# DeltaNet blocks and a mixture of experts on one core: five products on single heads in 64x64 tiles, and bulk transfers spread over the block

## The chip, the cores and the metric

The kernel runs on one core of a Trainium2 chip. The metric is the time of one execution on the device in microseconds; below, the median of several runs. The engines are called PE (matrix products, with PEld its weight loads), DVE (vector), ACT (scalar), POOL (GpSimd) and SP (which here only issues transfers). Each executes its instructions in the order of the program; they meet through semaphores.

## The reference, cut to what matters

```python
# q, k, v: (4, 8, 768, 48); beta: (4, 8, 768)
k_n = k / (norm(k) + 1e-6)
for t in range(S):
    y[t]  = q[t] @ state                       # state: 48 x 48 for each of 32 heads
    v_old = state.T @ k_n[t]
    state = state + beta[t] * outer(k_n[t], v[t] - v_old)
x = y as rows of 384                           # 3072 tokens
logits = x @ w_gate                            # 8 experts
expert = argmax(logits); gate_w = softmax(logits)[expert]
for e in range(8):                             # the 80 tokens of largest gate_w
    out[tok] = gate_w[tok] * (relu(x[tok] @ w1[e]) @ w2[e])
```

All other rows of the output are zero. All data are float32.

## The kernel before, in words

The sequence of 768 is cut into 12 chunks of 64 positions. `for j in range(NC)` (L766) makes one block of work of each; all 32 heads go through it together. A head has three numbers (e, p, g): e and p are 0 or 1, g is 0 to 7, and the tables of the chunk are laid out by them. In most operands one partition half (0 to 63, 64 to 127) holds heads of one e or one p, the other half those of the other.

Block j carries several chunks at different stages, so that the engines have work while the chain of the states runs:

- Chunk j, the chain. `chain_ks` (K times the state SB), `R` on DVE (V minus that, L474), `chain_tr` (the inverse factor YF times R), `UB` on DVE (the result times gam, L485), `chain_ku` (K times UB, added to the state in `S_ps`), and the copies of the state into SB on ACT (L504). Outputs: `chain_qs` (Q times the old state) and `chain_pu` (P times UB) add up in one PSUM tile, `x_out` copies it (L517) and stores it to `x_rows`, `out_t` transposes it and ACT copies it to xT (L528); `logits` of chunk j follow in block j+1.
- Chunk j+1, the inverse of a 64x64 triangular matrix per head, put together from 16x16 diagonal blocks: `place_y` (ACT), `merge_f` (B1 times XB), FB on DVE (L424), `merge_y`, the YF copies (L435), `merge_p`, the PB copies (L449, L451), `merge_u`, the YF copies of L464. `place_x(j+2)` (ACT, L408) makes XB for the next block.
- Chunks j+2 to j+5, the diagonal blocks. `gram(j+5)` on PE makes B1 and PT (L335, L340). `store(j+4)` writes B1's diagonal blocks to DRAM in eight transfers (L348), `fetch` brings them back as NT with one 16x16 block on each partition (L352). In odd blocks POOL inverts those of two chunks, `solve([j+3, j+4])` (L367 to L380). In the next, even block `put` writes the result to DRAM (L391) and `spread` brings it back as XD and YD, in four transfers (L402), for two chunks. XD is what place_x needs.
- Loads: `load_v(j+2)`, `load_kq(j+6)` (Q and K transposed, in two halves of 512 KB, into the buffer that chunk j has used), `load_k(j+8)`; in the last blocks `clear` (zeros into the output) and `load_first` (the first expert weights into free KQ buffers). `scale_v` (L319) multiplies V on POOL, `squares` and `norm` give the norms of K.
- `fill(us)` puts pieces of the routing work (`gate`, `gate_top`) between the others on DVE.

Nothing reorders this: the order of the calls in the block is the order on each engine, and SP takes its transfers in that order too, waiting for each one's semaphores before the next is issued.

Merge_f, chain_ks, chain_qs, chain_ku and chain_pu treat two heads with one product. The stationary side stacks both heads on 128 partitions, and the right side holds the two heads' 48 columns block by block, with zeros in between: 96 columns. For that SB, UB and XB carry an extra axis, whose other half is zeroed once at the start (L674). A float32 product counts as two matmul records, so such a product over 32 heads is 32 records. `chain_tr` and `gram` go through `tiles` (L222) instead: one head at a time on a quarter (64x64) of the array, the four quarters in turn. Every call of `mm` has line L234 in the profile, so products are told apart by their tiles.

After the blocks come the routing (thresholds, ranks, indices; 266 to 306 us in the profiled execution) and the eight experts (306 to 366 us), which the change leaves as they are.

Of the kernel before, what the change touches and what calls it, by code (L numbers as in the profile page):

```python
# [32 lines left out]
def _layout(inputs):  # L33
# [13 lines left out]
    out["vtok"] = vb.transpose(4, 0, 5, 3, 1, 2, 6).reshape(NC, 128, 16 * D)  # L47
# [30 lines left out]
def kernel(  # L78
# [85 lines left out]
    def load_first(s):  # L164
        t = KQ[s].rearrange("p g k w -> p (g k w)").rearrange("p (c f) -> p c f", f=F)
        for k in range(KW):
            e, c = divmod(s * KW + k, DK)
            w_t.setdefault(2 * e, []).append(t[:, k])
            nc.sync.dma_start(t[:, k], w1[e, :, c * F : c * F + F])

    with ExitStack() as actx:
# [19 lines left out]
        XB = blk.tile([128, NB, 2, 48], F32, name="XB")  # L191
        YB = blk.tile([128, NB, 2, 2, 16], F32, name="YB")
        FB = blk.tile([128, 2, 4, 2, 64], F32, name="FB")
        YF = fixed("YF", 2, [128, 2, 8, 64])
        PB_ = blk.tile([128, 2, 8, 32], F32, name="PB")
        SB = blk.tile([128, NQ, 2, 2, D], F32, name="SB")
        UB = blk.tile([128, NB, 2, D], F32, name="UB")
# [21 lines left out]
        PAIRS = [(a, 4 * c + ql) for a in range(2) for ql in range(4) for c in range(2)]  # L219
        XPAIRS = [(a, 4 * c + 2 * r + q) for a in range(2) for c in range(2) for q in range(2) for r in range(2)]  # L220

# [11 lines left out]
        def mm(out, lhsT, rhs, acc=False):  # L233
            nc.tensor.matmul(out, lhsT=lhsT, rhs=rhs, start=not acc, stop=not acc, skip_group_check=True)  # L234

# [51 lines left out]
        def norm_of(bs, ss):  # L287
# [22 lines left out]
            for i, c in enumerate(bs):  # L310
                for e in range(2):
                    for h in range(2):
                        nc.gpsimd.tensor_copy(nvs[hs(h), c, 8 * e : 8 * e + 8].rearrange("r (q p) -> r p q", p=2),
                                              nv[hs(e), i, :, h].rearrange("r (p q) -> r p q", p=2))
# [27 lines left out]
        def store(c, engs=(nc.sync, nc.sync)):  # L342
            if ok(c):
                ad = a_dram[c % 4].rearrange("(e g b r w) -> e b r g w", e=2, g=NB, b=4, r=16)
                for n in range(8):
# [58 lines left out]
        def place_x(c, es=(0, 1)):  # L404
            if ok(c):
                for e in es:
                    for i in range(3):
                        nc.scalar.mul(XB[hs(e), :, e, 16 * i : 16 * i + 16], XD[hs(e), :, c % 2], bmask[hs(e), i : i + 1])  # L408

# [8 lines left out]
        def merge_f(c, ps):  # L418
            if ok(c):
                for p, g in PAIRS:  # L420
                    mm(ps[hs(g // 4), p, 96 * (g % 4) : 96 * (g % 4) + 96].rearrange("r (e w) -> r e w", e=2),
                       B1[c % B1n][:, slot(p, g)], XB[:, slot(p, g)])
                for p in range(2):
                    nc.vector.copy_predicated(FB[:, p].rearrange("r g e w -> r (g e) w")[:, :, 0:48],  # L424
                                              mask48.bitcast(I32).unsqueeze(1).to_broadcast([128, 8, 48]),
                                              ps[:, p, :384].rearrange("r (g w) -> r g w", w=48))

        def merge_y(c, ps):
            if ok(c):
                for m in range(8):  # L430
                    for e in range(2):
                        mm(ps[hs(e), 0, 64 * m : 64 * m + 64], FB[:, m // 4, m % 4, e], YB[:, 8 * e + m].rearrange("r h b w -> r (h b w)"))
# [5 lines left out]
        def merge_p(c, ps, eng=None):  # L438
            if ok(c):
                for m in range(8):  # L440
                    for e in range(2):
                        for h in range(2):
                            k = 64 * h + 32 * (m % 2)
                            mm(ps[k : k + 32, 1, 128 * e + 32 * (m // 2) : 128 * e + 32 * (m // 2) + 32],
                               FB[64 * h + 32 : 64 * h + 64, m // 4, m % 4, e, 0:32], YF[c % 2][64 * h + 32 : 64 * h + 64, e, m, 32:64])
# [7 lines left out]
        def merge_u(c, ps):  # L453
            if ok(c):
                for m in range(8):
                    for e in range(2):
                        for h in range(2):
                            k = 64 * h + 32 * (m % 2)
                            mm(ps[k : k + 32, 0, 128 * e + 32 * (m // 2) : 128 * e + 32 * (m // 2) + 32],
                               FB[64 * h : 64 * h + 32, m // 4, m % 4, e, 0:32], PB_[64 * h : 64 * h + 32, e, m])  # L460
# [6 lines left out]
        def chain_ks(c, ps):  # L467
            if ok(c) and c > 0:
                kq = KQ[c % KQn]
                for e, g in PAIRS:  # L470
                    mm(ps[hs(g // 4), e, 2 * D * (g % 4) : 2 * D * (g % 4) + 2 * D].rearrange("r (p d) -> r p d", p=2),
                       kq[:, g, 0, hs(e)], SB[:, g, e])
                for e in range(2):
                    nc.vector.tensor_tensor(out=R[:, 8 * e : 8 * e + 8], in0=VT[c % VTn][:, 8 * e : 8 * e + 8],  # L474
                                            in1=ps[:, e, : 8 * D].rearrange("r (g d) -> r g d", d=D), op=Alu.subtract)

        def chain_tr(c, ps):
            if ok(c):
# [3 lines left out]
                                         Y[hs(g // 4), e, pq(p, g)], r[hs(g // 4), 8 * e + 2 * (g % 4) + p]))  # L482
                for e in range(2):
                    bt = gam[hs(e), c].rearrange("r (g c) -> r c g", c=2).unsqueeze(3).to_broadcast([64, 2, 8, D])
                    nc.vector.tensor_tensor(out=UB[hs(e), :, e].rearrange("r (g c) d -> r c g d", c=2),  # L485
                                            in0=ps[hs(e), :, : 8 * D].rearrange("r c (g d) -> r c g d", d=D), in1=bt, op=Alu.mult)

        def chain_qs(c, ps):
            if ok(c) and c > 0:
                kq = KQ[c % KQn]  # L490
                for e, g in XPAIRS:
                    mm(ps[hs(g % 4 // 2), g // 4, 4 * D * (g % 2) : 4 * D * (g % 2) + 4 * D]
                       .rearrange("r (p e d) -> r e p d", p=2, e=2)[:, e], kq[:, g, 1, hs(e)], SB[:, g, e],
                       acc=e + g % 2 > 0)

        def chain_ku(c):
            if ok(c) and c < NC - 1:
                kb = KT[c % KTn]
                for g in range(NQ):
                    for p in range(2):  # L500
                        mm(S_ps[hs(p, D), g // 4, 2 * D * (g % 4) : 2 * D * (g % 4) + 2 * D].rearrange("r (e d) -> r e d", e=2),
                           kb[:, slot(p, g)], UB[:, slot(p, g)], acc=True)
                for p in range(2):
                    nc.scalar.copy(SB[hs(p, D), :, :, p].rearrange("r (b g) e d -> r b (g e) d", b=2),  # L504
                                   S_ps[hs(p, D), :, : 8 * D].rearrange("r b (g d) -> r b g d", d=D))

        def chain_pu(c, ps):
            if not ok(c):
                return
            for p, g in XPAIRS:  # L510
                o = 4 * D * (g % 2) + 2 * D * p
                mm(ps[hs(g % 4 // 2), g // 4, o : o + 2 * D].rearrange("r (e d) -> r e d", e=2), PT[c % PTn][:, slot(p, g)], UB[:, slot(p, g)],
                   acc=c > 0)

        def x_out(c, ps, b):
            if ok(c):
                nc.scalar.copy(x_t[c % 2][:, b].rearrange("r h d -> r (h d)"), ps[:, b, : 8 * D])  # L517
# [137 lines left out]
        zr = out.rearrange("(a q r) d -> a q r d", q=128, r=2)  # L655

        def clear(a):
            if a < zr.shape[0]:
                nc.sync.dma_start(zr[a], zero.unsqueeze(1).to_broadcast([128, 2, DM]))
# [14 lines left out]
        for t in (YF[0], YF[1], XB, YB, SB, UB):  # L674
# [27 lines left out]
        nc.vector.tensor_copy(FB.rearrange("r p q e w -> r (p q e) w"), eye.unsqueeze(1).to_broadcast([128, NB, 64]))  # L702
# [49 lines left out]

        def gated(b, m0, m1):
# [12 lines left out]
        for j in range(NC):  # L766
            a, b2, m2 = pms[j % 2], pms[1 - j % 2], pms[2]
            store(j + 4)
            load_v(j + 2)
            place_y(j + 1)  # L770
            fetch(j + 4)
            if j % 2:
                scale_v(j + 1)
                squares(j + 6, SQ[0])
                squares(j + 7, SQ[1])
                scale_v(j + 2)
                solve([j + 3, j + 4])
            elif j == 0:
# [266 lines left out]
```

## Time and profile before

| | |
|---|---|
| median of 3 runs | 381.9 us (379.48 to 385.86) |
| the profiled execution | 376.49 us, its span 374.8 us |
| mean clock granted to PE | 0.858 |
| before block 1 (its chain_ks) | 0 to 71 us |
| blocks 1 to 11 | 71 to 266 us |
| PE waiting for XB (ACT, L408) | 14.9 us, 7 times |
| PE waiting for KQ to land | 14.0 us, 3 times |
| PE waiting with no releaser seen ("issue") | 9.5 us, 7 times |
| SP queue waiting for inv_blocks (L402) / for POOL's XY (L391) | 25.7 / 19.7 us |

A line of a timeline gives start, length, engine, line, operation, the tile written and those read, and how many instructions were merged; in brackets, how long the engine had been idle before and who released it. SPq and ACTq are transfers being issued by SP and ACT; their landing comes later. A line of the table by stretches gives each engine's busy time.

### The profile page before, as it was taken

Reading aid. Unit: us, or ns where it says so; the run is one execution under the profiler, and the core shown is the slowest. Engines: PE = TensorE matmul, PEld = TensorE weight load, DVE = VectorE, ACT = ScalarE, POOL = GpSimd, SP = SyncE. Lnnn points to the kernel's source line nnn. Section 1 sums busy time; section 2 is a strip of 40 time slices with the busy share of each in tenths; the row PEclk is TensorE's granted clock in tenths of the full one; section 3 lists DMA queues with packets and bytes.
Section 4 is the critical chain, followed back from the end, with each engine's and each line's share of the span. In section 5 each row is a group of like instructions: output and inputs, shape, how many; then the busy total and the mean of one; then the engine's idle time right before and its main releaser. Section 6 shows DMA issues by size and latency. Waiting matters only on the chain. (4 is left out here: it accounts for less than half of the span.)

```text
span 374.8 us, 16506 instructions
## 1 busy us (share of the span) xinstructions
PE 272.8 (73%) x7313; PEld 241.0 (64%) x7313; DVE 199.2 (53%) x489; ACT 159.7 (43%) x352; POOL 150.0 (40%) x377
## 2 busy tenths in 40 slices
PE   6334737748798978979987987697301579799994
PEld 2333427647697867978886977687301249799993
DVE  3699835518434969585464467575887720011111
ACT  3202557455566675757667487771200001111120
POOL 8366128905870588058705880100340052110001
PEclk9855687969698999698998599998855599999999
DMA  7786865396359646763468259927799527961000
GB/s 301 207 307 224 86 159 149 128 200 191 88 175 203 190 97 188 151 201 59 118 170 265 79 122 321 311 85 242 255 429 429 218 58 266 420 233 32 18 17 26
DMA packets 75879, 69.52 MB, mean 185 GB/s; under 512 B 57248, under 2 KB 65440, under 8 KB 73504
## 3 DMA queue, kind: packets, MB, share of 16 engines
q1 hardware_dynamic: 70080, 65.03, 55.8%
q10 hardware_dynamic: 4960, 1.48, 1.9%
q0 software_dynamic: 768, 1.97, 1.8%
q8 instruction: 57, 0.93, 1.0%
q14 instruction: 14, 0.11, 0.1%
HBM read 53.32 MB, written 15.14 MB: 183 GB/s over the span
## 5 line engine op out<-in xcount | busy, mean ns | idle before, releaser
L234 PE MATMUL pm<-KQ 48*64 48x128 f32 x704 | 29.0, 313 | 24.0 <-DMA KQ<-in_kqt_dram 14.0
L234 PE MATMUL pm<-SB,KQ 128*64 128x96 f32 x704 | 40.3, 275 | 6.0 <-ACT YF L464 5.0
L234 PEld LDWEIGHTS pm<-SB,KQ 128*64 128x64 f32 x704 | 35.8, 157 | 9.7 <-ACT YF L464 6.6
L234 PEld LDWEIGHTS pm<-KQ 48*64 48x64 f32 x704 | 23.6, 155 | 26.3 <-DVE XY L378 11.8
L319 POOL TENSOR_TENSOR VT<-VT,nvs 128x768 f32<-128x768 f32 x12 | 17.7, 1474 | 49.5 <-DMA VT<-in_vtok_dram 49.2
L408 ACT ACTIVATE XB<-XD,cst 64x256 f32<-64x256 f32 x72 | 31.2, 496 | 8.5 <-DMA XD<-inv_blocks 8.1
L376 POOL TENSOR_TENSOR tmpTrue<-XY,NT 128x28 f32<-128x28 f32 (+13 forms) x84 | 30.9, 368 | 6.1
L234 PE MATMUL pm<-XB,B 128*64 128x96 f32 x384 | 22.3, 279 | 14.9 <-ACT XB L408 14.9
L1003 ACT ACTIVATE hT<-hp 128x320 f32<-128x320 f32 x16 | 7.0, 437 | 61.3 <-PE hp L1000 61.3
L435 ACT COPY YF<-pm 64x256 f32<-64x256 f32 x48 | 17.6, 366 | 34.1 <-PE pm L234 31.3
L378 POOL TENSOR_TENSOR XY<-XY,tmpTrue 128x28 f32<-128x28 f32 (+13 forms) x84 | 28.0, 334 | 6.6
L234 PEld LDWEIGHTS pm<-XB,B 128*64 128x64 f32 x384 | 19.8, 160 | 16.1 <-ACT XB L408 15.6
L970 DVE COPY xTe<-xp 128x240 f32<-128x240 f32 x8 | 3.3, 408 | 50.1 <-PE xp L968 50.1
L1011 PE MATMUL yp<-hT,w 128*64 128x80 f32 x768 | 29.1, 234 | 0.4 <-issue 0.4
L424 DVE COPY_PREDICATED FB<-cst,pm 128x384 f32<-128x384 int32 x24 | 12.8, 588 | 30.5 <-PE pm L234 30.5
L1011 PEld LDWEIGHTS yp<-hT,w 128*64 128x64 f32 x768 | 27.5, 137 | 2.1 <-issue 1.0
L984 POOL DMA_INDIRECT out_dram<-y,idx_s x8 | 7.4, 920 | 52.2 <-DVE y L983 52.2
L485 DVE TENSOR_TENSOR UB<-pm,gam 64x768 f32<-64x768 f32 x24 | 22.9, 955 | 3.2 <-PE pm L234 2.7
L474 DVE TENSOR_TENSOR R<-VT,pm 128x384 f32<-128x384 f32 x22 | 11.2, 551 | 23.9 <-PE pm L234 9.4
L335 DVE TENSOR_TENSOR B<-pm,ngam 128x512 f32<-128x512 f32 x22 | 15.1, 690 | 15.0 <-PE pm L234 14.0
L414 ACT ACTIVATE YB<-YD,cst 64x256 f32<-64x256 f32 x48 | 21.7, 498 | 0.5
L464 ACT COPY YF<-pm 32x256 f32<-32x256 f32 x24 | 8.7, 363 | 24.6 <-DVE YF L464 15.5
(177 smaller groups left out, 595.8 us busy)
## 6 DMA issues: line engine op xcount, KB each, us to landing
w<-in_w_dram SPq DMA_DIRECT2D x12, 1536.0 KB, 12.3
KQ<-in_kqt_dram SPq DMA_DIRECT2D x6, 1024.0 KB, 7.6
KQ<-in_kqt_dram SPq DMA_DIRECT2D x12, 512.0 KB, 5.6
KQ<-in_w_dram SPq DMA_DIRECT2D x12, 512.0 KB, 6.3
VT<-in_vtok_dram SPq DMA_DIRECT2D x12, 384.0 KB, 4.1
x_rows<-x SPq DMA_DIRECT2D x12, 384.0 KB, 5.1
out_dram<-zero SPq DMA_DIRECT2D x12, 384.0 KB, 4.7
KT<-in_ktok_dram SPq DMA_DIRECT2D x11, 384.0 KB, 7.8
```

The lines of the kernel that those rows point to most:

```text
L234: nc.tensor.matmul(out, lhsT=lhsT, rhs=rhs, start=not acc, stop=not acc, skip_group_check=True)
L319: eng.tensor_tensor(out=V, in0=V, in1=nvs[:, c].unsqueeze(2).to_broadcast([128, NB, D]), op=Alu.mult)
L335: nc.vector.tensor_tensor(out=own(B1[c % B1n], h), in0=pv[:, 0], in1=own(ngam[:, c].unsqueeze(2).to_broadcast([128, NB, 64]), h), op=Alu.mult)
L376: eng.tensor_tensor(out=tv, in0=X[:, :, t + 1 :, t : t + 1].to_broadcast(sh), in1=NT[:, :, 0:t, t].unsqueeze(2).to_broadcast(sh), op=Alu.mult)
L378: eng.tensor_tensor(out=X[:, :, t + 1 :, 0:t], in0=X[:, :, t + 1 :, 0:t], in1=tv, op=Alu.add)
L408: nc.scalar.mul(XB[hs(e), :, e, 16 * i : 16 * i + 16], XD[hs(e), :, c % 2], bmask[hs(e), i : i + 1])
L414: nc.scalar.mul(YB[hs(h), :, h, b], YD[hs(h), :, c % 2], bmask[hs(h), 2 * b + 1 : 2 * b + 2])
L424: nc.vector.copy_predicated(FB[:, p].rearrange("r g e w -> r (g e) w")[:, :, 0:48], mask48.bitcast(I32).unsqueeze(1).to_broadcast([128, 8, ...
L435: nc.scalar.copy(YF[c % 2][hs(h), e].rearrange("r m (b x w) -> r m b x w", b=2, x=2)[:, :, :, 1], ps[hs(e), 0].rearrange("r (m h b w) -> r ...
L474: nc.vector.tensor_tensor(out=R[:, 8 * e : 8 * e + 8], in0=VT[c % VTn][:, 8 * e : 8 * e + 8], in1=ps[:, e, : 8 * D].rearrange("r (g d) -> ...
L485: nc.vector.tensor_tensor(out=UB[hs(e), :, e].rearrange("r (g c) d -> r c g d", c=2), in0=ps[hs(e), :, : 8 * D].rearrange("r c (g d) -> r ...
L1011: nc.tensor.matmul(yp[r, d * cap : (d + 1) * cap], lhsT=w2_t[f][:, d * 128 + 64 * n : d * 128 + 64 * n + 64], rhs=hT[:, f, :], start=(f == ...
```

## The change

It has four parts.

1. The five products go through `tiles`, one head at a time, 48 columns wide: 64 records for 32 heads. SB, UB and XB lose the extra axis. SB gets two buffers, used in turn by the chunks. V, FB and the sums in PSUM are laid out to suit. The operations on DVE and ACT that fill these tiles cover 128 partitions at once.
2. `chain_qs` is cut in two halves of 16 heads; the first is issued before chain_tr, the second after chain_pu.
3. Of the eight stores of a chunk's diagonal blocks, four are issued by ACT. `fetch` follows right behind `load_v`; `put` moves from behind chain_qs to the start of the block; `spread` moves behind chain_pu. In odd blocks `scale_v` no longer stands around squares and ahead of solve; both chunks are scaled in even blocks.
4. The two halves of a KQ load are issued in different places: the first half late in block j, the second early in block j+1; the expert weights that go into the KQ buffers likewise. `clear` works on pieces of half the size, three in each block from block 4 on, in three places, instead of two in each block from block 6 on.

```diff
-        XB = blk.tile([128, NB, 2, 48], F32, name="XB")
+        XB = blk.tile([128, NB, 48], F32, name="XB")
-        SB = blk.tile([128, NQ, 2, 2, D], F32, name="SB")
-        UB = blk.tile([128, NB, 2, D], F32, name="UB")
+        SB = fixed("SB", 2, [128, 2, NQ, D])
+        UB = blk.tile([128, NB, D], F32, name="UB")
...
+        def xmm(row, ps, ops, acc, heads=HEADS):
+
+            seen = set()
+
+            def emit(e, p, g):
+                t = g % 4 // 2, e
+                o = D * (4 * (g // 4) + 2 * (g % 2) + p)
+                mm(ps[hs(t[0]), e, o : o + D], *ops(e, p, g), acc=acc or t in seen)
+                seen.add(t)
+
+            tiles(lambda e, p, g: (row(e, p), g % 4 // 2), emit, heads)
...
-        def place_x(c, es=(0, 1)):
-            if ok(c):
-                for e in es:
-                    for i in range(3):
-                        nc.scalar.mul(XB[hs(e), :, e, 16 * i : 16 * i + 16], XD[hs(e), :, c % 2], bmask[hs(e), i : i + 1])
+        def place_x(c):
+            if ok(c):
+                for i in range(3):
+                    nc.scalar.mul(XB[:, :, 16 * i : 16 * i + 16], XD[:, :, c % 2], bmask[:, i : i + 1])
...
-                for p, g in PAIRS:
-                    mm(ps[hs(g // 4), p, 96 * (g % 4) : 96 * (g % 4) + 96].rearrange("r (e w) -> r e w", e=2),
-                       B1[c % B1n][:, slot(p, g)], XB[:, slot(p, g)])
+                tiles(lambda e, p, g: (e, g // 4),
+                      lambda e, p, g: mm(ps[hs(g // 4), e, 48 * pq(p, g) : 48 * pq(p, g) + 48],
+                                         B1[c % B1n][hs(e), slot(p, g)], XB[hs(e), slot(p, g)]))
...
-                for e in range(2):
-                    bt = gam[hs(e), c].rearrange("r (g c) -> r c g", c=2).unsqueeze(3).to_broadcast([64, 2, 8, D])
-                    nc.vector.tensor_tensor(out=UB[hs(e), :, e].rearrange("r (g c) d -> r c g d", c=2),
-                                            in0=ps[hs(e), :, : 8 * D].rearrange("r c (g d) -> r c g d", d=D), in1=bt, op=Alu.mult)
+                for h in range(2):
+                    bt = own(gam[:, c].unsqueeze(2), h).to_broadcast([128, 8, D])
+                    nc.vector.tensor_tensor(out=own(UB, h), in0=ps[:, h, : 8 * D].rearrange("r (m d) -> r m d", d=D), in1=bt, op=Alu.mult)
...
-        def chain_qs(c, ps):
+        def chain_qs(c, ps, k):
             if ok(c) and c > 0:
                 kq = KQ[c % KQn]
-                for e, g in XPAIRS:
...
+                xmm(lambda e, p: p, ps, lambda e, p, g: (kq[hs(p, D), g, 1, hs(e)], SB[c % 2][hs(p, D), e, g]), k > 0,
+                    [hd for hd in HEADS if hd[0] ^ hd[1] != k])
...
+        def load_kq_or_w(c, p):
+            if KQn <= c < NC:
+                load_kq(c, parts=(p,))
+            elif NC < c < NC + KQn:
+                load_first(c - NC - 1, (p,))
...
         for j in range(NC):
             a, b2, m2 = pms[j % 2], pms[1 - j % 2], pms[2]
-            store(j + 4)
+            store(j + 4, (nc.sync, nc.scalar))
             load_v(j + 2)
+            fetch(j + 4)
+            load_kq_or_w(j + 5, 1)
+            clear(3 * j - NC)
+            if j % 2 == 0:
+                put([j + 2, j + 3])
             place_y(j + 1)
-            fetch(j + 4)
             if j % 2:
-                scale_v(j + 1)
                 squares(j + 6, SQ[0])
                 squares(j + 7, SQ[1])
+                solve([j + 3, j + 4])
+            else:
+                if j == 0:
+                    squares(6, SQ[0], nc.scalar)
+                scale_v(j + 1)
                 scale_v(j + 2)
-                solve([j + 3, j + 4])
-            elif j == 0:
-                squares(6, SQ[0], nc.scalar)
-                scale_v(1)
             chain_ks(j, a)
             logits(j - 1, m2)
...
             merge_f(j + 1, b2)
+            chain_qs(j, a, 0)
             chain_tr(j, m2)
-            chain_qs(j, a)
-            if j % 2:
-                load_kq(j + 6)
-            else:
-                put([j + 2, j + 3])
-                load_kq(j + 6, parts=(0,))
-                spread(j + 2)
-                load_kq(j + 6, parts=(1,))
             merge_y(j + 1, b2)
...
             chain_ku(j)
             load_k(j + 8)
-            if j >= NC // 2:
-                clear(2 * j - NC)
-                clear(2 * j - NC + 1)
-                if j > NC - KQn:
-                    load_first(j - 1 - NC + KQn)
...
             chain_pu(j, a)
+            chain_qs(j, a, 1)
+            load_kq_or_w(j + 6, 0)
+            if j % 2 == 0:
+                spread(j + 2)
+            clear(3 * j - NC + 1)
             lists(m2)
             x_out(j, a, 0)
...
             x_out(j, a, 1)
+            clear(3 * j - NC + 2)
...
             if j % 2:
-                place_x(j + 2, (0,))
+                place_x(j + 2)
                 out_t(j, m2)
-                place_x(j + 2, (1,))
             else:
                 out_t(j, m2)
                 place_x(j + 2)
```

Chain_ks, chain_ku and chain_pu change in the manner of merge_f.

## The prediction

> **What bounds the kernel now.** I read first the page's busy times, then a table of busy time by stretches, one per block, then the timelines of the engines in one pair of blocks, and the issue-to-landing times of the tiles on the way. The page:
>
> ```profile
> PE 272.8 (73%) x7313; PEld 241.0 (64%) x7313; DVE 199.2 (53%) x489; ACT 159.7 (43%) x352; POOL 150.0 (40%) x377
> ```
>
> No engine is full. The chain that ended last covers only the final 8 us, so the blocks are read singly. The stretches of blocks 5 and 6 (columns: busy us and instructions per engine, granted clock, DMA share, GB/s):
>
> ```profile
> core 0: us, PE busy (x) PEld busy (x) DVE busy (x) ACT busy (x) POOL busy (x), PEclk, DMA share, GB/s
> 153.00:172.30 19.30, 16.91 (x479) 15.51 (x478) 12.11 (x28) 13.27 (x30) 8.67 (x20) 0.85 0.56 158
> 172.30:187.80 15.50, 15.05 (x481) 13.64 (x480) 7.38 (x16) 10.64 (x23) 11.75 (x31) 0.98 0.46 101
> ```
>
> TensorE looks nearly full. Inside block 6 the products run back to back (PE timeline; start, length):
>
> ```profile
> 174.59 1.54 PE L234 MATMUL pm<-XB,B 128*64 128x96 f32 x32
> 176.06 1.15 PE L234 MATMUL pm<-R,YF 64*64 64x48 f32 x64
> 177.14 1.54 PE L234 MATMUL pm<-SB,KQ 128*64 128x96 f32 x32
> 178.51 1.10 PE L234 MATMUL pm<-YB,FB 128*64 128x64 f32 x32
> ```
>
> From start to start, a 128-row product takes 1.37 to 1.47 us, while chain_tr, already in 64x64 tiles, does the same heads in 1.08.
>
> But a second thing runs round each pair of blocks. SP, POOL, ACT and PE timelines, odd block 5 to odd block 7:
>
> ```profile
> 152.60 6.17 SPq L348 DMA_DIRECT2D a_blocks<-B  x8
> 158.81 0.45 SPq L263 DMA_DIRECT2D VT<-in_vtok_dram  x1
> 160.12 0.34 SPq L352 DMA_DIRECT2D NT<-a_blocks  x1
> 179.35 0.37 SPq L391 DMA_DIRECT2D inv_blocks<-XY  x1
> 183.58 1.91 SPq L402 DMA_DIRECT2D XD<-inv_blocks  x2
> ```
> ```profile
> 162.47 1.47 POOL L319 TENSOR_TENSOR VT<-VT,nvs 128x768 f32<-128x768 f32 x1 [13.52 <-DMA VT<-in_vtok_dram]
> 163.90 1.66 POOL L367 TENSOR_TENSOR XY<-NT,cst 128x256 f32<-128x256 f32 x2
> 178.10 1.21 POOL L380 COPY XY<-XY 128x256 f32<-128x256 f32 x2
> ```
> ```profile
> 188.61 2.61 ACT L408 ACTIVATE XB<-XD,cst 64x256 f32<-64x256 f32 x6
> ```
> ```profile
> 191.27 1.54 PE L234 MATMUL pm<-XB,B 128*64 128x96 f32 x32 [1.27 <-ACT XB L408]
> ```
>
> Block 5 stores its diagonal blocks, fetches them as NT, POOL solves (163.9 to 179.3, 15.4 us), the result goes out and comes back as XD, ACT makes XB, and merge_f of block 7 waits for it: 38.7 us from first store to merge_f. Two blocks and the 3.4 us to merge_f give the same. So TensorE and this chain are balanced, at 17.35 us a block ((255.15 - 116.35)/8, from ks of block 3 to ks of block 11). In block 1 the chain is worse: XD lands at 77.5, PE waits 7.0 us, and the store starts only at 79.07, behind the spread on SP's queue.
>
> **What the skill says.** "TensorEngine Tiling (Array Packing)", Key Properties: tiles execute weight loads and matmuls in parallel, and a change of tiling mode drains the array. The trace agrees with the first: 1.08 us for 64 instructions is 17 ns each, against 46 for a 128-row one; no row shows the drain alone. "DMA: Bandwidth & Descriptors", Issuing engines are not separate DMA queues: issuing from more engines saves only issue time. That fits the stores here: 0.45 us median to issue on SP, 0.46 on ACT. "Runtime: NRT & Kernel Launch", Instruction fetch mechanics: instructions come in 16 KiB blocks of 256 by DMA. The trace agrees: 57 packets, 0.93 MB on the instruction queue.
>
> **The change, part by part.**
>
> *TensorE.* merge_f 1.47, ks 1.47, qs 1.37, ku 1.32 and pu 1.42 sum to 7.05 us. As 64 single-head instructions each, I take 1.08 (chain_tr's row), 1.0 for ku, whose weights have 48 columns: 5.3. That is 1.75 us less a block. Bounds: no gain in any (the tiles serve one another badly), or 0.74 each, as the 64 32x32 instructions of merge_p run.
>
> *Vector and Scalar.* UB: two ops of 768 columns at 0.955 become two of 384; by R's row 0.55 each, so 1.94 becomes 1.15. SB copies: 1.61 becomes 0.96 (x's row, 128x384). XB: six ops in 2.61 become three of 128x256; YF L416 does two in 0.91, so 1.37. Three POOL memsets of 1.38 go; POOL waits 11.7 us for NT just after, so they are worth nothing.
>
> *QS in two parts.* Half of qs no longer covers UB. After tr only merge_y (0.93) stands before ku, and UB takes 1.15 and 0.1 of latency: 0.3 us of new waiting a block. SB gets a second buffer, so the late half of qs does not hold the next state.
>
> *The block that results.* ks 1.08, logits 0.82, f 1.08, qs half 0.54, tr 1.08, y 0.93, wait 0.3, ku 1.0, pu 1.08, qs half 0.54, p 0.75; gram's half 1.03 covers the PB copies all but 0.25, u 0.75, gram 1.03, out_t 0.9: 13.2 us. ACT then holds some 12 us a block, its four store issues included.
>
> *The queues.* Four of eight stores go to ACT. Behind them on ACT is place_y, so merge_y waits for them; in even blocks by about 0.2, in odd ones by about 1. But in odd blocks they stand behind place_x, which waits for XD. This closes a loop: XD lands, XB, ACT's stores, NT, solve, out, XD. In the old order the store did not wait for XB. scale_v leaves the way: POOL waited there for VT and spent 1.47 before the solve. The put moves ahead of SP's waits for TensorE. KQ's second half and one clear now stand on SP between fetch and put (issue 0.45 and 0.6), hidden by the 15.4 us solve. The last KQ half issues some 6 us into a block and lands after 6.2 (median), against a use at 11 to 12: just covered; uncovered it costs PE up to 1 us, inside the slack below. Clears double in number and halve in size: 12 more issues of SP, off the way.
>
> *The loop's length.* XB 1.37; ACT's stores 3 x 0.46 and 2.8 to landing, 4.2; NT 2.7; solve 15.4; gap to put 0.1; put to the first XD issue 3.9 (69.41 to 73.70, 143.97 to 147.27, 179.35 to 183.58); second XD issue 0.6 and 3.7 to landing: 32.0 us a pair, more than the 2 x 13.2 of the engines. So the loop decides; TensorE stands some 4 us a pair, and loses about 1.5 more to a cold clock after it, which fits into the slack.
>
> *Sum.* XD still lands at 77.3 the first time (the solve that ends at 69.4 is untouched). Then 109.3, 141.3, 173.3, 205.3, and merge_f of block 9 starts 1.4 later, at 206.7; now it is at 226.3: 19.6 saved. From there the loop is over. From merge_f of block 9 to that of block 10 now 16.6; with y ending 3.65 after merge_f, UB's end at 3.9, DVE's filler of 4.5 behind it, YF on DVE and ACT 1.6, next ks 1.1, and ACT's place_x and xT 2.2 before logits 0.8: 12.9, so 3.7 saved. Block 10's merge_f to ks of block 11: 12.3 becomes 10.1. Block 11 saves 1.5 (UB 0.8, ks 0.4, half of qs less its latency). 19.6 + 7.4 = 27. The expert stage after it (306 to 366, PE 57.5 of 60 busy) isn't touched, and its weights start as much earlier.
>
> The profiled execution took 376.5 us (span 374.8): 349.5. The median shown is 381.9, 1.4% above it: 354.5, say 355. About 2% is what a measurement of this kernel tells from no change.
>
> **Rivals.**
>
> *The loop is shorter and the engines decide.* With every landing at the least seen (stores 1.7, NT 2.0, put 2.2, XD 2.7) the loop is 28, against 26.4 plus 1.5 for a cold clock. For it: transfers are spaced, and the DMA share is about half. Against: medians include quiet stretches already. Four loops of 28 put merge_f at 190.7; 376.5 - 35.6 - 7.4 = 333.5 by the profile, 338 by the median.
>
> *ACT's stores wait.* Each reuses a DMA semaphore whose earlier transfer (x_rows 5.1 us, KQ 5.6) may be in flight; ACT's longest store issue was 1.15 us. With 0.75 more per store the loop is 35: merge_f at 218.7, 7.6 + 7.4 saved, 361.5 and 367. For it: SP's eight stores took 3.8 to 6.6 us for this reason.
>
> *Little happens:* both the stores and the loads' landings lengthen the loop to 38, no gain there, only the last three blocks' 7: 370 and 375.
>
> *Slower: TensorE starves for instructions.* 478 matmuls a block become 638, with weight loads 1276 instructions, 5.0 fetches. Every fetch stands among bulk packets. With the cold clock a block is 13.95 us of work; it takes 18.5 us a block for eight blocks to eat the first loop's gain of 9, so 0.9 us exposed per fetch decides. At 1.2, blocks take 20: +21 - 9, 388 and 394. For it: gram waited 3.4 us for "issue" at 92.8 with the DMA share at 90%. Against: all such waits of PE are 9.5 us in 57 fetches, 0.17 each.
>
> **How the numbers follow.** Loop decides 0.52 (own range 347 to 363); engines decide 0.15; ACT's stores wait 0.20; little 0.06; starved 0.07. Low end 340: most of the second case stays in. High end 372: the third is in. Left out: little, starved and a bit of the second, under 0.2. Faster 0.87, same 0.06, slower 0.07.
>
> **What would show it.** Right: the five products at 64x48 in about 1.1 us; UB ops near 0.55; merge_f's waits for XB in odd blocks 3 to 9 of 2 to 5 us, none in even ones; solves starting 32 us apart; ACT's stores right behind XB. Wrong: PE waits for "issue" above 1 us in most blocks; solves 35 or more apart; or no PE wait for XB at all.

## The result, and the profile after

The change made the kernel slower: 417.8 us median (415.42 to 421.29, four runs) against 381.7 us (379.48 to 385.86) on the same chip, a ratio of 1.095 with a 95% interval of 1.088 to 1.102. Some executions of most kernels here are one or two per cent slower than the others; medians count them, ratios leave them out, and the profiled executions of pad160 and wide_logits below were such ones. The prediction was 355 us. The profiled execution took 421.29 us, its span is 419.6 us.

The page after, busy times:

```profile
PE 305.7 (73%) x9137; PEld 269.6 (64%) x9137; DVE 180.7 (43%) x489; ACT 135.5 (32%) x316; POOL 146.4 (35%) x374
```

DVE and ACT work 19 and 24 us less. PE issues a quarter more matmul records and is busy 33 us longer, though its products are smaller: the mean granted clock (1 is full speed) fell from 0.858 to 0.696. Two blocks in the middle, from merge_u to merge_u (columns as in the prediction):

```profile
158.02:180.23 22.21, 18.54 (x639) 17.04 (x639) 10.21 (x28) 9.95 (x25) 5.28 (x16) 0.63 0.54 142
180.23:205.42 25.19, 18.98 (x641) 17.16 (x641) 7.03 (x15) 10.28 (x24) 15.36 (x36) 0.66 0.44 116
```

They take 22 and 25 us, where the two shown of before took 19.3 and 15.5, at a clock of 0.63 and 0.66. From logits to logits the ten intervals from chunk 0 to chunk 10 take 21.8 us in the mean, 18.5 before. Inside one block (PE timeline):

```profile
155.93 0.80 PE L231 MATMUL pm<-YF,FB 32*32 32x32 f32 x63 [1.99 <-issue]
156.66 1.35 PE L231 MATMUL pm<-KQ 48*64 48x128 f32 x32
158.02 0.68 PE L231 MATMUL pm<-PB,FB 32*32 32x32 f32 x33
161.03 0.67 PE L231 MATMUL pm<-PB,FB 32*32 32x32 f32 x31 [2.32 <-issue]
161.63 1.99 PE L231 MATMUL pm<-KQ 48*64 48x128 f32 x32
...
170.88 1.92 PE L231 MATMUL pm<-R,YF 64*64 64x48 f32 x64
...
174.58 0.94 PE L231 MATMUL S_ps<-UB,KT 64*48 64x48 f32 x64
175.33 1.11 PE L231 MATMUL pm<-UB,PT 64*64 64x48 f32 x64
176.26 0.65 PE L231 MATMUL pm<-SB,KQ 48*64 48x48 f32 x32
176.84 0.21 PE L231 MATMUL pm<-YF,FB 32*32 32x32 f32 x1
178.13 0.80 PE L231 MATMUL pm<-YF,FB 32*32 32x32 f32 x63 [1.08 <-issue]
```

The reader is to look at the counts. The first stall shown ends at 155.93, the second comes after 63 + 32 + 33 = 128 records, in the middle of a run of equal products, with nothing on any engine to wait for. The third follows 510 records later by the trace (31 + 32 + 6 + 64 + 24 + 64 + 32 + 64 + 32 + 64 + 64 + 32 + 1), which is 4 x 128 but for two; records missing from the trace, or instructions of PE that are no products, would account for them. So it goes on through the blocks: but for a drift of a few records, the stalls stand 128 records or a multiple of it apart. Each float32 record has its weight load beside it (x9137 on PE, x9137 on PEld), so that is every 256 instructions. The lines of the waits, and after them the instruction queue of PE before and after (packets, MB, share):

```profile
PE pm L231 <- issue: 36.6, 23, 4.0
PE pm L231 <- ACT XB L415: 6.6, 2, 3.4
```
```profile
q8 instruction: 57, 0.93, 1.0%
```
```profile
q8 instruction: 71, 1.16, 1.2%
```

9137 - 7313 = 1824 records more, with their weight loads 3648 instructions, are 14.25 times 256; the queue carries 14 packets more, of 16 KB each. The waits with no releaser were 9.5 us in 7 pieces before. The operations that the change makes smaller did become so (DVE and ACT groups; after the bar busy us and mean ns):

```profile
L491 DVE TENSOR_TENSOR UB<-pm,gam 128x384 f32<-128x384 f32 x24 | 12.3, 552 | 19.7 <-PE pm L231 19.7
```
```profile
L415 ACT ACTIVATE XB<-XD,cst 128x256 f32<-128x256 f32 x36 | 15.7, 498 | 6.7 <-DMA XD<-inv_blocks 6.5
L505 ACT COPY SB<-S_ps 128x384 f32<-128x384 f32 x22 | 9.5, 482 | 0.3
```

And the loop of the diagonal blocks isn't late any more; POOL waits for work in each odd block (waits of POOL):

```profile
POOL XY L375 <- DMA NT<-a_blocks: 70.6, 5, 18.6
```

Of the 44.8 us that the span grew, 3.1 lie before the logits of chunk 0; from those to the logits of chunk 1 5.1 are saved (29.4 to 24.3 us); the nine intervals up to chunk 10 cost 38.1, the last one 2.4; and 6.2 came after the blocks.

### The profile page after: what moved, and what is told of

It reads as the page before. It is cut to its first block, busy times and chain, and to the rows that moved or that the text cites. A ratio compares the mean times of both kernels' runs of the same rounds, so it can differ in the third digit from the quotient of the medians.

```text
span 419.6 us, 20127 instructions
## 1 busy us (share of the span) xinstructions
PE 305.7 (73%) x9137; PEld 269.6 (64%) x9137; DVE 180.7 (43%) x489; ACT 135.5 (32%) x316; POOL 146.4 (35%) x374
## 5 line engine op out<-in xcount | busy, mean ns | idle before, releaser
L231 PE MATMUL pm<-KQ 48*64 48x128 f32 x704 | 33.4, 350 | 17.6 <-DMA KQ<-in_kqt_dram 12.8
L231 PE MATMUL pm<-SB,KQ 48*64 48x48 f32 x1408 | 42.0, 287 | 4.0 <-issue 2.6
L231 PEld LDWEIGHTS pm<-SB,KQ 48*64 48x64 f32 x1408 | 38.0, 204 | 5.3 <-ACT YF L470 3.0
L231 PEld LDWEIGHTS pm<-KQ 48*64 48x64 f32 x704 | 27.2, 177 | 19.7 <-DVE XY L386 11.9
L375 POOL TENSOR_TENSOR XY<-NT,cst 128x256 f32<-128x256 f32 x11 | 9.3, 853 | 77.0 <-DMA NT<-a_blocks 70.6
L231 PE MATMUL pm<-XB,B 64*64 64x48 f32 x768 | 23.6, 301 | 8.6 <-ACT XB L415 6.6
L231 PEld LDWEIGHTS pm<-XB,B 64*64 64x64 f32 x768 | 21.4, 216 | 10.1 <-ACT XB L415 6.8
L231 PE MATMUL pm<-PB,FB 32*32 32x32 f32 x768 | 13.9, 221 | 18.0 <-issue 15.5
L231 PEld LDWEIGHTS pm<-PB,FB 32*32 32x32 f32 x768 | 11.3, 130 | 21.4 <-issue 16.3
L231 PE MATMUL pm<-YF,FB 32*32 32x32 f32 x768 | 11.8, 202 | 17.0 <-issue 13.1
```

Source lines behind the costliest of these rows:

```text
L375: eng.tensor_tensor(out=X[:, i], in0=NT[:, i].rearrange("p s t -> p t s"), in1=low16, op=Alu.mult)
```

## The experiments

The theory that this profile suggests, called F (instruction supply): PE's instructions arrive in blocks of 256, one every few microseconds; a product in tiles uses its block faster than the next one comes, and the change raises the number of blocks per chunk from 3.7 to 5.0. Its rivals were Q (the new order of the transfers did it), C (the low clock did it, and the stalls are a by-product), and F1 (the fetches are only slow because the bulk transfers stand beside them). The recorded expectations of p_only and q_only call F "theory P"; that of no_bulk calls it F2. All times below are medians beside the kernel before on the same chip (379.99 to 383.44 us). "Issue" is PE's idle time without a releaser in blocks 0 to 11, from the PE timeline; the last column is 120 us divided by the records that PE executed between 100 and 220 us, for 128 of them.

| kernel | records a block | time, us | ratio (95%) | clock | issue, us | us per 128 records |
|---|---|---|---|---|---|---|
| before | 478 | 381.7 | | 0.858 | 9.6 | 4.87 |
| after | 638 | 417.8 | 1.095 (1.088 to 1.102) | 0.696 | 37.2 | 4.45 |
| p_only | 638 | 421.4 | 1.114 (1.104 to 1.123) | 0.735 | 43.5 | 4.46 |
| q_only | 478 | 383.4 | 1.007 (1.003 to 1.011) | 0.847 | 9.0 | 4.90 |
| heat8 | 646 | 426.2 | 1.127 (1.117 to 1.137) | 0.799 | 50.7 | 4.76 |
| no_bulk | 638 | 402.6 | 1.059 (1.046 to 1.073) | 0.737 | 30.6 | 4.07 |
| half16 | 478 | 376.2 | 0.992 (0.988 to 0.996) | 0.696 | 21.0 | 4.83 |
| pad160 | 638 | 426.0 | 1.124 (1.109 to 1.139) | 0.782 | 27.0 | 4.61 |
| pad80 | 558 | 399.6 | 1.044 (1.037 to 1.051) | 0.807 | 7.0 | 4.64 |
| wide_logits | 466 | 387.3 | 1.000 (0.995 to 1.004) | 0.848 | 8.1 | 4.93 |
| lean | 434 | 385.9 | 1.001 (0.996 to 1.005) | 0.860 | 4.8 | 5.51 |
| f_tiles | 498 | 385.7 | 1.004 (1.000 to 1.008) | 0.852 | 15.7 | 4.61 |

The waits for issue alone don't rank the kernels: half16 has 21.0 us of them and loses nothing, pad80 has 7.0 and is 4.4% slower. PE's work between the waits counts as well.

**p_only** and **q_only**: each part of the change alone. p_only is the kernel after with the loads, stores, put, spread and clears in the order of before; q_only is the kernel before with those in the order of after.

```diff
--- after, p_only
-            store(j + 4, (nc.sync, nc.scalar))
+            store(j + 4)
...
-            fetch(j + 4)
-            load_kq_or_w(j + 5, 1)
-            clear(3 * j - NC)
-            if j % 2 == 0:
-                put([j + 2, j + 3])
```

> The products in tiles and QS in two parts as in the change, but the order of all transfers, scale_v and clears as before. Theory P (the tile products themselves cost the time, by running out of instructions at the edges of 256-instruction blocks and by the low clock that follows): 405 to 425, PE waits for issue over 20 us in the blocks, clock about 0.7. Rival Q (the new places of the bulk transfers cost it): 350 to 372.

> The products as before, but the order of all transfers, scale_v and clears as in the change. Theory P: 360 to 382, clock 0.84 or more, PE waits for issue under 12 us. Rival Q: 395 or more, with issue waits where KQ and clear are issued, beside merge_p.

Measured: 421.4 and 383.4 us. The products in tiles, with QS in two parts, are the whole loss. The new order of the transfers costs the kernel before 0.3 to 1.1%; beside the tiles it may help a little (1.114 without it, 1.095 with it, on different chips). Q falls.

q_only doesn't decide whether the loop of the diagonal blocks held the kernel before: with the new order the solves start 36.9, 34.6 and 42.1 us apart, against 37.8, 35.4 and 37.8 before, so the loop did not get shorter there. The trace of before says more. Its waits of ACT for XD, and what stands on ACT ahead of the XB operation of block 7 (188.61 in the prediction's lines):

```profile
ACT XB L408 <- DMA XD<-inv_blocks: 8.1, 2, 5.8
```
```profile
187.91 0.80 ACT L528 COPY xT<-pm 128x768 f32<-128x768 f32 x1 [0.60 <-PE pm L527]
```

ACT waits for XD only twice, both times before block 2. In block 7 it was free for XB only when it had copied xT, and for that it had waited for PE's out_t; XD had landed by then. So from block 2 on PE's waits for XB (3.4 us in 5) were not waits for XD, the end of the loop.

**heat8**: eight bf16 products of 128x512 ahead of each chain_ks, to keep the clock up.

```diff
+            if j > 0:
+                heat(8, a)
             chain_ks(j, a)
```

> The changed kernel with eight more bf16 128x128 products of 512 columns ahead of chain_ks in each block from 1 on (16 instructions, no part of the result). If the low clock from ks to merge_y is what costs most (theory C), they bring it up: clock 0.85 or more, ks to merge_y shorter by 4 us a block, less 1.8 to 3.4 for themselves: 385 to 405. If the supply of instructions is the limit (theory F), the tiles then run into more edges at full speed: issue waits rise from 36 to 50 us or more and the time stays within 410 to 430.

Measured: 426.2 us at a clock of 0.799. The four groups of products on XB, SB, R and UB (all but chain_ku) fell from 102.7 to 80.1 us of busy time, and the added products took some 29. But PE's waits for issue rose from 37 to 51 us. Of the 22.6 us that the products win by the clock, 13.5 come back as stalls; by these numbers a warm clock that cost nothing would be worth some 9 of the 36 us lost, an estimate. That speaks against C as the main cause, but the time rose, so it is not a clean test; half16 below is the stronger one.

**no_bulk**: the kernel after without the KQ loads from chunk 6 on and without the zeros in the output, the first expert weights loaded behind the blocks. The later chunks work on older Q and K and the output isn't zeroed; the amount of work on PE is the same.

```diff
-            if 0 <= a < zr.shape[0]:
+            if False:
                 nc.sync.dma_start(zr[a], zero)
...
         def load_kq_or_w(c, p):
-            if KQn <= c < NC:
-                load_kq(c, parts=(p,))
-            elif NC < c < NC + KQn:
-                load_first(c - NC - 1, (p,))
+            return
```

> The changed kernel without the KQ reloads from chunk 6 on, without the clears, and with the first expert weights loaded only after the blocks (so chunks 6 to 11 work on older Q and K, and the output is not zeroed). Theory F1 (instruction blocks arrive late because they stand among bulk packets): issue waits in the blocks fall under 12 us, clock above 0.8, blocks at 16 us or less. Theory F2 (a block of 256 instructions takes longer to fetch than the tiles take to use it, with or without bulk): issue waits stay above 20 us, blocks at 19 us or more. The late weight loads may add up to 10 us after the blocks; the blocks are what counts.

Measured: 402.6 us, the DMA rate between 100 and 220 us 100 instead of 142 GB/s, 4.07 us per 128 records instead of 4.45, and still 26 stalls. From logits to logits it takes 20.2 us in the mean, against 21.8 in the kernel after and 18.5 before, so the late weights are not what keeps it slow. The bulk transfers lengthen the fetches, but without most of them the kernel is still 22 us slower than the one before. F1 holds for a part only. (What the kernel before would gain without them was not tried.)

**half16**: the five products read the upper 16 bits of each number as bf16, so that each takes one record and one weight load instead of two and two. The lower 16 bits are left out; data, tiles, DVE, ACT and the transfers stay.

```diff
+        def top(x):
+            return x.bitcast(BF16)[:, 1::2]
+
+        def mm16(out, lhsT, rhs, acc=False):
+            nc.tensor.matmul(out, lhsT=top(lhsT), rhs=top(rhs), start=not acc, stop=not acc, skip_group_check=True)
```

> The changed kernel, but its five products read only the upper 16 bits of each float32 (as bf16), so that a head takes two instructions instead of four: the 64x64 tiles and all other parts stay, the instructions of TensorE per block fall from 1276 to about the 956 of before (the products are less exact). Theory F (a block of 256 instructions comes only every 4 us or so): as fast as before or faster, 350 to 380, issue waits under 15 us in the blocks, clock above 0.8. Theory C (64x64 tiles of 48 columns themselves do not keep the clock up, whatever their instructions): clock stays near 0.7, 395 or more.

Measured: 376.2 us, 0.8% under the kernel before and, by the two ratios, 9% under the kernel after. With the number of records back at 478 a block (57 packets on the instruction queue, as before), the loss is gone, at a clock as low as after's (0.696) and with all of the change's tiles and transfers in place. Theory C expected this clock, but with 395 us or more. Theory F was wrong in two points: it expected a clock above 0.8, and waits for issue under 15 us instead of 21.0. The run takes PE time away with the records (247.8 us busy instead of 305.7), so it doesn't show the count alone; the next two add records with little work.

**pad160** and **pad80**: the kernel before with 80 or 40 tiny products ahead of each chain_ks from block 1, which leave its results alone.

```diff
+            if j > 0:
+                for i in range(80):
+                    r = k = 32 * (i % 4)
+                    mm(a[k : k + 32, 0, 0:2], ident[r : r + 32, r : r + 32], ident[r : r + 32, 0:2])
             chain_ks(j, a)
```

> The kernel before with 80 tiny float32 products (32x32 by 2 columns, 160 records, 320 instructions, no part of the result) ahead of chain_ks in each block from 1 on: as many instructions as the change adds, with next to no work. Theory F: 410 to 435, issue waits of 30 us and more in the blocks. If only what they run for counts (about 12 ns each, 1.9 us a block, twice that at half clock): 395 to 408 at most, issue waits under 20 us.

> The kernel before, with 40 tiny products (32x32x2, 80 records, about 1 us of work) ahead of chain_ks in blocks 1 to 11: half of the padding of pad160, 880 records, 6.9 blocks of 256 instructions. Instruction supply, linear from the first record: half of pad160's 46 us, +23 us, 403 us, PE's issue waits in the blocks about half way from 9.6 to 27 us. Instruction supply with slack in the kernel before (some fetches still hidden): the first 80 records cost clearly less than the second 80, under +15 us. Only the work of the padding on PE counts: +1.0 us a block, +11 us, and no change in the issue waits.

Measured: 426.0 and 399.6 us; by the executions that the ratios use, 46.9 and 17.7 us over the kernel before. What the padding itself takes (groups of PE, pad80 and pad160):

```profile
L234 PE MATMUL pm<-cst 32*32 32x2 f32 x880 | 11.7, 175 | 9.0 <-issue 3.3 <-ACT YF L464 3.2 <-DVE og L608 2.2
```
```profile
L234 PE MATMUL pm<-cst 32*32 32x2 f32 x1760 | 24.9, 183 | 17.8 <-issue 12.9 <-ACT YF L464 4.7
```

Of pad80's 17.7 us, 11.7 are the padding's own time, and its waits for issue didn't grow (7.0 us): the first 80 records cost 6 us more than their work. The expectations had under 15 us with slack and 23 without, so this run lies between them. Of pad160's 46.9 us only 24.9 are the padding's own, and the waits for issue are 17 us more, if fewer than the 30 us that F expected. The second 80 records cost 29 us, the first 18. This points to some slack in the kernel before that ends between 558 and 638 records a block. The clock plays into it too: it is 0.782 in pad160 and 0.807 in pad80 instead of 0.858, and PE's other products are busy 22 and 19 us longer; how much of the time is owed to that was not separated.

**micro_quiet** and **micro_loaded**: nothing of the reference, only rows of equal float32 products, in the first with no transfer beside them, in the second under 48 loads of 1.5 MB (423 GB/s); each was executed once.

```diff
-    for i in range(0):
+    for i in range(48):
         nc.sync.dma_start(W[i % 4], w1[i % 8])
```

> No part of the computation: TensorE alone runs long rows of 64x64x48 tiles (cold and after a warm-up), 128x64x96 products, 32x32x32 tiles and again 128x64x96 from cold, with no transfers of data in the main part. Theory F: rows of tiles stop at every 128th record; the time from one edge to the next is the time of one fetch, 2.5 to 4 us, and is the same for 64x64 and 32x32 tiles; 128x64x96 (46 ns each, 5.9 us per 128) does not stop. Theory F1 (fetches are slow only among bulk packets): no stops at all here, 17 ns per record of 64x64.

> As the run before, with 48 loads of 1.5 MB going on beside it. Theory F: the time from edge to edge grows, to 4 to 7 us, and the 128x64x96 rows may begin to stop as well. If bulk transfers do not delay instruction fetches: as in the quiet run.

PE timelines; first micro_quiet:

```profile
46.80 2.08 PE L124 MATMUL pa<-L,G 64*64 64x48 f32 x128 [1.38 <-issue]
50.25 2.08 PE L124 MATMUL pa<-L,G 64*64 64x48 f32 x128 [1.38 <-issue]
53.71 2.08 PE L124 MATMUL pa<-L,G 64*64 64x48 f32 x128 [1.38 <-issue]
...
110.28 31.90 PE L130 MATMUL pb<-L,G 128*64 128x96 f32 x768
...
163.54 1.92 PE L135 MATMUL pa<-L,G 32*32 32x32 f32 x128 [1.53 <-issue]
166.99 1.93 PE L135 MATMUL pa<-L,G 32*32 32x32 f32 x128 [1.53 <-issue]
```

and micro_loaded:

```profile
45.48 3.66 PE L124 MATMUL pa<-L,G 64*64 64x48 f32 x128 [2.54 <-issue]
51.68 3.66 PE L124 MATMUL pa<-L,G 64*64 64x48 f32 x128 [2.53 <-issue]
...
186.03 5.50 PE L130 MATMUL pb<-L,G 128*64 128x96 f32 x128 [0.48 <-issue]
192.22 5.50 PE L130 MATMUL pb<-L,G 128*64 128x96 f32 x128 [0.70 <-issue]
...
220.94 1.93 PE L135 MATMUL pa<-L,G 32*32 32x32 f32 x128 [1.53 <-issue]
224.39 1.92 PE L135 MATMUL pa<-L,G 32*32 32x32 f32 x128 [1.53 <-issue]
```

This measures the disputed thing alone. But for the first and last stretch of each, the rows break at exactly 128 records. From edge to edge it takes 3.45 us at the least in quiet (up to 4.0), whether the product is 64x64x48 or 32x32x32, though 128 of them are done in 2.1 or 1.9 us. A 128-row product takes 31.90/6 = 5.3 us per 128 and never stops. Under load the edge to edge is 5.9 to 6.5 us, mostly 6.2, for the tile and for the wide product alike; in the same run, when the loads are over (from about 200 us on), it is 3.45 again. So it isn't a property of tiles: it is a shortest time for 256 instructions, 3.45 us in quiet and about 6.2 us under that load. The kernel after stands between them with 4.45.

**wide_logits**, **lean** and **f_tiles** ask the other way: is there something to win with fewer records, or with one product in tiles and few records? wide_logits has the kernel before with 12 records less in logits; lean also pairs chain_tr with zeros in R, as the other products were; f_tiles is wide_logits with merge_f alone in tiles.

```diff
--- wide_logits
-                        for n in range(2):
-                            nc.tensor.matmul(pl[hs(n), b, :E], lhsT=xT[:, b, j, hs(n)],
-                                             rhs=wg[:, j, :], start=(j == 0), stop=(j == DK - 1), skip_group_check=True)
+                        nc.tensor.matmul(pl[:, b, :E], lhsT=xT[:, b, j],
+                                         rhs=wg[:, j, :], start=(j == 0), stop=(j == DK - 1), skip_group_check=True)
--- lean, besides
-        R = blk.tile([128, NB, D], F32, name="R")
+        R = blk.tile([128, NB, 2, D], F32, name="R")
...
+                            mm(ps[hs(e), m // 4, 2 * D * (m % 4) : 2 * D * (m % 4) + 2 * D].rearrange("r (h d) -> r h d", h=2),
+                               Y[:, e, m], R[:, 8 * e + 2 * (m % 4) + m // 4])
--- f_tiles, besides wide_logits
-        XB = blk.tile([128, NB, 2, 48], F32, name="XB")
+        XB = blk.tile([128, NB, 48], F32, name="XB")
...
+                tiles(lambda e, p, g: (e, g // 4),
+                      lambda e, p, g: mm(ps[hs(g // 4), e, 48 * pq(p, g) : 48 * pq(p, g) + 48],
+                                         B1[c % B1n][hs(e), slot(p, g)], XB[hs(e), slot(p, g)]))
```

> The kernel before, with the logits' products on 128 columns of the stationary side instead of two of 64: 12 records fewer a block (466 instead of 478), the same output. Instruction supply, linear below the kernel before as well: 132 records, 1.03 blocks of instructions at 3.3 us, so 3.4 us less, 378 us, ratio 0.991. Slack in the kernel before: no change within 1 us. Loop of the diagonal blocks: no change.

> wide_logits, and chain_tr in the manner of the other products (two heads stacked on 128 partitions, R block by block with zeros, so that 32 records do what 64 did): 434 records a block instead of 478; R's two DVE operations become 64x768 (0.95 us each instead of 0.55), the product itself 1.4 instead of 1.08 us. The zeros for the output come from a smaller tile, and the warm-up products read another buffer. The same output. Instruction supply, linear: 484 records, 3.8 blocks of instructions, 12.5 us less, against at most 1.15 us more work a block on the chain of the states (12.7 us if all of it is exposed, 0 if the supply decides in every block): 369 to 382 us. Slack in the kernel before: only the added work shows, 382 to 394 us.

> The kernel before with one of the five products, merge_f, on single heads in 64x64 tiles (XB three operations of 128x256 on ACT in 1.3 us instead of six in 2.6; 32 records more a block), and the logits of wide_logits (12 records fewer): 498 records a block, still below the count at which pad80 (558) and pad160 (638) began to cost. The same output. Instruction supply with slack up to about 550 records: nothing lost by the 20 records, and 0.35 us of PE and 1.3 us of ACT a block gained where they are on the path: 375 to 382 us. Instruction supply, linear: 220 records more, 1.7 blocks of instructions, +5.7 us, less 0.35 us a block, 384 us. Loop of the diagonal blocks, as the prediction had it: 1.24 us less a pair of blocks, five pairs, 6 us less, 376 us; the run can't tell this from the first, only from the second.

Measured: ratios 1.000, 1.001 and 1.004, no difference in any. wide_logits excludes the 0.9% that a linear price of records would give: below 478 records nothing is to be had, which fits the slack that pad80 points to. lean can't say more, since fewer records and more work may cancel; that its added work cost nothing visible fits a chain of the states with room in it. f_tiles is inconclusive between "nothing lost" and the linear price (384 us, 1.005); it doesn't show the 6 us that a shorter XB would give if it stood on the path. No version beat the kernel before within float32.

## Why the prediction was wrong

The step that failed is the term for instruction fetches. The main sum, 13.2 us of work in a block, has none; the rival "Slower: TensorE starves for instructions" had the mechanism and the 5.0 fetches a block, and was given 0.07 because of its sentence "Against: all such waits of PE are 9.5 us in 57 fetches, 0.17 each." Measured were 21.8 us a block, with 37.2 us of such waits in the blocks; 5.0 fetches of 3.45 to 6.2 us each are 17 to 31 us a block, an estimate from the two micro runs. The 0.17 us is a mean over fetches most of which were hidden: 128 records of the kernel before take 4.87 us, longer than most fetches beside its transfers, so what its trace shows is what sticks out of a fetch under slow products, not how long one takes. The profile had one of the numbers for the right question: 1.08 us for 64 records in tiles is 2.2 us for 128, against a fetch time of which the trace showed only that it is mostly under 4.9. The Trainium skill's page "Runtime: NRT & Kernel Launch", Instruction fetch mechanics, holds the fetch to be mostly hidden, behind the time that issuing the instructions takes. The runs differ, and decide: 3.45 us for 256 instructions in quiet are 13.5 ns each, a product in tiles uses them at 8.1 ns (2.08 us for 256). The rival's price, 0.9 us exposed per fetch, was not the right one either: the kernel after shows about 0.6 (37.2 us in some 60 fetches) and lost all the same, because between the stalls its products ran at a lower clock and PE was busy 33 us longer.

By the prediction's other steps:

- *Five products 7.05 to 5.3 us.* The row of chain_tr was a good price for the arithmetic at full clock: ku 0.75, pu 0.93 and half of qs 0.58 from start to start were measured where the clock was 1.00 (predicted 1.0, 1.08 and 0.54). It was no price for five of them in a row. Alone between wide products, chain_tr used 128 of 256 instructions of a block fast and the rest slowly; with its neighbours in tiles too, no slow products are left to fetch behind.
- *About 1.5 us a pair for a cold clock.* Mis-sized. From the stall at 158.7 to 161.0 on the products run at half speed until about 173: ks, f and tr take 1.74 to 1.89 us from start to start instead of 1.08, and 12 us at half clock are some 6 us lost in this one block, an estimate. Part of that time covers fetches (heat8: with the clock up, 13.5 us more of stalls), so it is not simply to be added to the stalls.
- *UB, SB, XB.* Right: 0.552 us for a UB operation (0.55 predicted), 0.86 for two SB copies (0.96), 1.31 for XB (1.37). They lie on DVE and ACT, beside a PE that waits for instructions, and so are worth nothing.
- *The loop decides, 32.0 us a pair.* Wrong: the solves start 41 to 46 us apart (86.8, 128.2, 174.0, 218.6 us), two blocks; after block 1's 3.4 us PE waits for XB in no block from 2 to 11. That XB waited for the loop in the kernel before was misread: from block 2 on ACT never waits for XD there. The two equal times (38.7 us round the loop, and two blocks plus 3.4) were no proof: a loop that is fed by the blocks takes as long as they do.
- *The first loop saves 9 us.* 5.1 by the logits.
- *ACT's stores.* Right so far as the runs go: behind XB; ACT waits 3.4 us in all for stores ahead of YB, and PE never waits for YB.
- *The expert stage isn't touched.* Its code isn't, yet 6.2 us of the growth lie behind lt_ps, with 4.1 us in 6 "issue" waits of hp. Under the weight loads a fetch of 6.2 us would do that, but p_only has 4.1 us of issue waits there and before has 2.0; what moved the weight loads against these products was not tried.

What stays open: what ended last in the kernel before. Not the loop from block 2 on (ACT's waits for XD), and not the supply of instructions alone (wide_logits, lean). Open too is why the clock falls so far in the kernel after (half16 has the same clock and no loss); that the stalls bring it down is argued from their place ahead of the slow stretch, not shown by a run of its own.

## What to carry to other kernels

Before small tiles replace wide products, count instructions, not only their time: records and weight loads per stage, divided by 256, times the shortest time of an instruction block (3.45 us in quiet, about 6.2 under full load here), are a floor under the stage, to be compared with the work that each 256 instructions do. Waits with "issue" as their releaser that lie a fixed number of instructions apart were fetches here; their mean over all fetches said nothing of what one costs, because most of them don't show. And a resource that shows little waiting in the trace of before must be priced by its own period under the new demand, best by a row of equal instructions measured alone.

## What the runs showed that was not expected

- 256 instructions of PE take at least 3.45 us in quiet and 5.9 us, mostly 6.2, beside 423 GB/s of loads (micro_quiet, micro_loaded). In the blocks, with about half of the DMA time in use, no kernel here that keeps the bulk transfers went below 4.45 us per 128 records.
- A wide product can be hit too: under full load the 128x64x96 row, 5.50 us for 128 records, waits 0.48 to 0.70 us at each edge.
- The clock: in micro_quiet, with a stall of 1.38 us in every 3.45, the granted clock stays at 1.00 under 64x64x48 tiles (43 to 105 us), but it is 0.56 under 32x32x32 tiles with 1.53 us of stall in the same 3.45 (149 to 172 us). In micro_loaded, with 2.5 to 3.1 us of stall in 6.2, it is 0.57 on average (33 to 89 us). In the kernel after one stall of 2.3 us was followed by some 12 us at half clock. So the length of the stalls alone doesn't give the clock.
- A float32 product of one head costs four instructions, two records and two weight loads; read as bf16 it costs two (half16: 160 records a block fewer, 14 instruction packets fewer).
